# Values of two attention steps computed in one go in every second step, with four transposed-weight buffers and five MLP-input buffers

## The chip, the cores and the metric

The kernel runs on one core of a Trainium2 chip. The core has TensorE (PE, matrix products; PEld in the profile is its weight load), VectorE (DVE), ScalarE (ACT), GpSimd (POOL) and SyncE (SP), which here issues every DMA. The metric is the device time of one execution in microseconds (us), lower is better. The time before is the median of three runs.

## The reference

Two blocks follow each other. The first is attention with eight heads over a batch of eight, in which each query keeps only its 32 largest scores; the second is an MLP with a smooth ReLU.

```python
def _attn_ref(q, k, v):                   # (8, 8, 576, 64) each
    top_k = 32
    scores = scale * np.matmul(q, k.transpose(0, 1, 3, 2))
    kth = np.partition(scores, -top_k, axis=-1)[..., -top_k:-top_k + 1]
    scores = np.where(scores >= kth, scores, -1000000000.0)
    scores = scores - np.max(scores, axis=-1, keepdims=True)
    attn = np.exp(scores)
    attn = attn / (np.sum(attn, axis=-1, keepdims=True) + 1e-09)
    return np.matmul(attn, v).astype(np.float32)

def _moe_ref(x, w_in, w_out):             # (4608, 512), (512, 2048), (2048, 512)
    h = x @ w_in
    beta = 1.0
    neg = h <= -beta
    pos = h >= beta
    g = np.where(pos, h, np.where(neg, 0.0, (h + beta) ** 2 / (4.0 * beta)))
    return (g @ w_out).astype(np.float32)
```

Between them the attention's output is laid out as one row of 512 numbers (8 heads of 64) for each of the 8 x 576 tokens. Everything is float32.

## The kernel before

**Steps.** The attention is cut into 144 steps. One step takes a tile of 128 queries and two heads: 128 x 2 x 576 scores. A tile of queries needs four steps for its eight heads. The 576 queries of a batch element make four full tiles and a tail of 64; the tails of two batch elements share one tile of the MLP, and each tail takes two steps of four heads. The batch elements go in pairs: four tiles of the first, its tail, the tail of the second, four tiles of the second; so 36 steps a pair. A tile that has all its heads is a *chunk* for the MLP; there are 36 chunks.

**What one step does, engine by engine.** `scores` (L333) multiplies queries and keys on TensorE into PSUM (`sp`), and ScalarE evicts them to `s` (L352). VectorE finds the 32nd largest (`more`, `less`, MAX8 and MATCH_REPLACE8, L354 to L446) and multiplies the exponentials `e`, which ScalarE made (L388), with the mask (L451). GpSimd divides by the sum (L404). The weights must then be transposed, since the values are multiplied with the weights' columns on the partitions. In the early steps TensorE does it (`transpose_w`, L460); later `move_w` (L477) does it with DMAs: ScalarE splits the words into 16-bit halves (L481), SP writes them to DRAM (`rows`, L483) and reads them back transposed into a `wT` buffer (L484). There are three `wT` buffers. `values` (L490) multiplies values and `wT` on TensorE, 20 matmuls in the source (16 of `v_in`, 4 of the tail, as the profile counts them) into a PSUM tile `po`, and ScalarE copies `po` into `xT` (L511), the input of the MLP. When a chunk has its last values, `mlp` (L522) puts its pieces on a list.

**The MLP's pieces.** A chunk has eight pieces `hidden` (`ph`, L531: 16 matmuls in the profile for two blocks of hidden units; ScalarE makes `r` and `g` from `ph`, L535 and L542, GpSimd finishes `g`, L547 to L549) and sixteen `final` (`py`, L554), each four pieces behind its `hidden`. `ph` and `po` have one tag, so that both rotate through the same three PSUM buffers. `advance` (L625) puts pieces between the attention's instructions, as many as a planned share and a planned time of TensorE allow.

**Order.** The instructions on TensorE, VectorE, ScalarE and GpSimd stand exactly in the order in which this program issues them; each engine takes them in that order and waits where an operand is not ready or a buffer is not free. Only SP's order is the framework's. The main loop (L727) goes through steps `m` in seven slots. While the weights of the MLP are still being converted to the form in which the kernel keeps them (`early`, steps 0 to 8), other rules hold. Afterwards step `m` issues: in slot 1 the turning of queries for step `m + 3` (and in every second step a part of the next keys), in slot 2 the values of step `m - 3` and then the scores of step `m + 2`, in slot 3 the moving of the weights of step `m - 1`:

```python
                if slot == 2 and not early:
                    values_until(m - 2)
                if slot == (4 if early else 2):
                    begin_at(m + 2)
```

`values_until(x)` (L715) issues the values of all steps below `x` that are not issued yet. So before the change there is one set of values and one set of scores in each step, one behind the other on TensorE. The values of a chunk's last head pair always belong to an odd step.

**Buffers.** The pool `xtp` (L177) has six `xT`. A query tile is loaded into one of two `q_in`, and a tail into one `q_tl` of its own (L204 to L211). From the second batch pair on, queries are turned through DRAM as well: ScalarE makes `parts`, SP writes `lines` and reads them back transposed as `qT` or, for a tail, `qTt` (L272 to L279).

Of the kernel before, what the change touches and what calls it, by code (L numbers as in the profile page):

```python
# [11 lines left out]
F32 = mybir.dt.float32  # L12
# [14 lines left out]
def kernel(  # L27
# [11 lines left out]
    B, H, S, D = q.shape  # L39
    NTOK, DM = out.shape  # L40
    DFF = moe_w_in.shape[1]
    P = 128
# [6 lines left out]
    TL = S - SM  # L49
    assert 2 * TL == P  # L50
    SH = S // 2
    BLOCKS = 2 * NT + 1
# [121 lines left out]

    def run(ctx, paired):
        unit = 2.0 if paired else 1.0
        xtp = ctx.enter_context(tc.tile_pool(name="xtp", bufs=6))  # L177
        stage = ctx.enter_context(tc.tile_pool(name="stage", bufs=2))
        att = ctx.enter_context(tc.tile_pool(name="att", bufs=2))
        dram = ctx.enter_context(tc.tile_pool(name="dram", bufs=3, space=bass.MemoryType.DRAM))  # L180
# [3 lines left out]
        def whole(x, b):  # L184

            return x[b, :, 0:SM, :].rearrange("h (p c) d -> p h c d", c=NT)
# [17 lines left out]
        def load_queries(b, t):  # L204
            if t < NT:
                q_in = stage.tile([P, H, D], F32, name="q_in", bufs=2)
                nc.sync.dma_start(out=q_in, in_=whole(q, b)[:, :, t, :])
            else:
                q_in = stage.tile([TL, H, D], F32, name="q_tl", bufs=1)
                nc.sync.dma_start(out=q_in, in_=q[b, :, SM:S, :].rearrange("h p d -> p h d"))  # L210
            return q_in  # L211


        def main(i):
            return slice(0, SM) if i == 0 else slice(TL, S)

        def tail(i):
            return slice(SM, S) if i == 0 else slice(0, TL)
# [240 lines left out]

        def transpose_w(st):  # L460
            w = st["e"]
            st["wT"] = wT = (late or words).tile([P, BLOCKS, P], F32, name="wT", bufs=3 if late else 1)
            pt = ps.tile([P, 2, NT, P], F32, name="pw", tag="a", bufs=2)
            for i in range(2):
                for c in range(NT):
                    nc.tensor.matmul(pt[:, i, c, :], w[:, i, main(i)][:, c * P:(c + 1) * P], st["rz"][:, i, :],  # L466
                                     start=True, stop=True)
            for i in range(2):
                nc.scalar.copy(wT[:, i * (NT + 1):i * (NT + 1) + NT], pt[:, i])  # L469
            pt = ps.tile([P, P], F32, name="pwt", tag="a", bufs=2)  # L470
            for i in range(2):
                nc.tensor.matmul(pt[i * TL:(i + 1) * TL, :], w[:, i, tail(i)], st["rz"][:, i, :], start=True, stop=True)
            nc.scalar.copy(wT[:, NT], pt)
# [1 line left out]


        def move_w(st):  # L477
            st["wT"] = wT = late.tile([P, BLOCKS, P], F32, name="wT", bufs=3)
            halves = late.tile([P, 2, 2 * S], U16, name="halves")
            for i in range(2):  # L480
                nc.scalar.copy(halves[:, :, i * S:(i + 1) * S], st["e"][:, i, :].bitcast(U16).rearrange("p (k t) -> p t k", t=2))  # L481
            rows = dram.tile([P, 2, 2 * S], U16, name="rows")
            nc.sync.dma_start(out=rows, in_=halves)  # L483
            nc.sync.dma_start_transpose(wT.bitcast(U16), rows.rearrange("p t k -> (p t) k"))  # L484
# [31 lines left out]
        def rows_of(b, t):  # L516
            r0 = b * S
            if t < NT:
                return [(0, P, out[r0:r0 + SM, :].rearrange("(p c) n -> p c n", c=NT)[:, t, :])]
            return [(i * TL, (i + 1) * TL, out[r0 + i * S + SM:r0 + (i + 1) * S, :]) for i in range(2)]  # L520
# [74 lines left out]
        words, late = conversion.enter_context(tc.tile_pool(name="words", bufs=1)), None  # L595
# [19 lines left out]
        def inspect():  # L615
            nonlocal inspected
            if paired and inspected < n_pieces:
                inspect_piece(late, inspected)
                inspected += 1
# [67 lines left out]
        def begin_at(m):  # L687
            nonlocal pe_time
            if m < n:
                queries(m)  # L690
                begin(m)
                pe_time += 1.15
                scored[m] = pe_time + 2.0
# [21 lines left out]
        def values_until(m):  # L715
            nonlocal valued, pe_time
            while valued < min(m, n):
                pe_time = max(pe_time, ready_at[valued]) + 1.25
                values(state[valued])
                state[valued] = None  # L720
                if valued in ready:
                    ch = ready[valued]
                    mlp(xTs[ch], rows_of(*chunks[ch]), mlp_pool, ch == len(chunks) - 1)
                valued += 1

        first_late = None
        for m in range(n + 2):  # L727
            early = converted < n_pieces
            if not early and first_late is None:
                first_late = m  # L730
            elif not early and late is None:
                conversion.close()
                room.clear()
                late = ctx.enter_context(tc.tile_pool(name="late", bufs=1))

            share, left = (total - spent) / (n + 2 - m), sum(x[0] for x in pending)
            for r in sorted(ready):
                if r + 4 > m and r >= valued:
                    share = min(share, left / (r + 4 - m))
                    left += NK * NF + NF * DM // P  # L740
            top_k, parts = None, [0] * SLOTS
            if m < n:
                top_k = weights(state[m], state[m - 1] if m > 0 else None, state[m + 1] if m + 1 < n else None)
                parts = [1] * SLOTS if early else [1, 1, 0, 1, 1, 1, 1]
                start = max(dve_time, scored[m])
                now_converting = range(SLOTS)
                dve_time = start + K_TIME + PIECE_TIME * min(len(now_converting), n_pieces - converted)
                done[m] = dve_time
                state[m]["by_tensor"] = early or m >= n - 2
            for slot in range(SLOTS):  # L750
                now = start + (dve_time - start) * (slot + 1) / SLOTS
                for _ in range(parts[slot]):
                    next(top_k, None)
                if m < n and converted < n_pieces:
                    if slot in now_converting:
                        convert(now)
                elif slot == 3 and late is not None:
                    if m % 2:
                        inspect()
                    elif paired:  # L760
                        load(late, inspected, 1)
                if slot == 1 and 1 <= m <= n and state[m - 1]["by_tensor"]:
                    pe_time = max(pe_time, done[m - 1] + 2.0) + 1.0
                    transpose_w(state[m - 1])
                    ready_at[m - 1] = pe_time + 1.8
                if slot == 3 and 1 <= m <= n and state[m - 1] is not None and not state[m - 1]["by_tensor"]:
                    move_w(state[m - 1])
                    ready_at[m - 1] = done[m - 1] + 15.0
                if slot == 2 and m == n and paired:
                    judge(ps, att)  # L770
                if slot == 2 and (early or m == first_late or m >= n - 1):
                    values_until(m)
                if m == 0 and slot in (1, 2):
                    next(first)
                if slot == 2 and not early:
                    values_until(m - 2)
                if slot == (4 if early else 2):
                    begin_at(m + 2)
                if slot == (6 if early else 1):
                    queries(m + 3)  # L780
                    if (m < n and prep is None and next_keys < B and steps[m][0] == next_keys - 1 and steps[m][1] >= 1
                            and (next_keys > 1 or converted == n_pieces)):
                        prep = (turned_keys_of if next_keys > 1 else keys_of)(next_keys)
                    if prep is not None and (m % 2 == 0 or next_keys == 1):
                        got = next(prep, None)
                        pe_time += 0.5 if next_keys < 2 else 0.0
                        if got is None:
                            prep, next_keys = None, next_keys + 1
                        else:
                            keys[next_keys] = got  # L790
                advance((EARLY_SHARE if early else share) / SLOTS if m < n else 32.0, now)
            for _ in (top_k if top_k is not None else ()):
                pass
# [50 lines left out]
```

## Time and profile before

| | us |
|---|---|
| median of the runs | 1522.77 |
| all three runs | 1517.87, 1522.77, 1523.53 |
| the execution that was profiled | 1522.56 |
| its span, first to last instruction | 1520.5 |

The mean granted TensorE clock in the profiled execution is 0.981 of full speed. The stages are: up to about 130 us the MLP's weights are loaded and converted beside the first steps; from there to about 1440 us attention and MLP run side by side; the rest is MLP alone.

The costliest groups on each engine, from the same page (busy time, mean of one):

| engine, line, what | count | busy us | mean ns |
|---|---|---|---|
| PE L531 `ph` (hidden) | 4608 | 557.4 | 276 |
| PE L554 `py` (final) | 1152 | 550.7 | 603 |
| PE L351 `sp` (scores, 64x288) | 1024 | 163.6 | 436 |
| PE L498 `po` (values, `v_in`) | 2048 | 143.5 | 280 |
| DVE L372 MATCH_REPLACE8 | 864 | 375.0 | 437 |
| DVE L451 mask times `e` | 288 | 266.6 | 959 |
| POOL L404 division | 266 | 248.7 | 945 |
| POOL L549 end of `g` | 280 | 242.1 | 865 |
| ACT L481 `halves` | 266 | 293.6 | 1144 |

How to read it: a line of the timeline gives start and length of a run of equal instructions and, in brackets, the idle time of the engine before it with what ended that. Lengths of matmuls overlap, since matmuls are pipelined; the starts tell how long a group holds TensorE. A wait line gives total, count and longest. A line of windows gives the busy time of each engine in a stretch, with the number of instructions or groups in brackets, then the granted clock, the share of time in which the DMA engines moved data, and GB/s.

### The profile page before, as it was taken

Reading aid. Unit: us, or ns where it says so; the run is one execution under the profiler, and the core shown is the slowest. Engines: PE = TensorE matmul, PEld = TensorE weight load, DVE = VectorE, ACT = ScalarE, POOL = GpSimd, SP = SyncE. Lnnn points to the kernel's source line nnn. Section 1 sums busy time; section 2 is a strip of 40 time slices with the busy share of each in tenths; the row PEclk is TensorE's granted clock in tenths of the full one; section 3 lists DMA queues with packets and bytes.
Section 4 is the critical chain, followed back from the end, with each engine's and each line's share of the span. In section 5 each row is a group of like instructions: output and inputs, shape, how many; then the busy total and the mean of one; then the engine's idle time right before and its main releaser. Section 6 shows DMA issues by size and latency. Waiting matters only on the chain.

```text
span 1520.5 us, 32206 instructions
## 1 busy us (share of the span) xinstructions
PE 1450.9 (95%) x10625; PEld 1041.8 (69%) x10625; DVE 1422.2 (94%) x4424; ACT 1171.0 (77%) x2288; POOL 942.7 (62%) x1339
## 2 busy tenths in 40 slices
PE   5588999999999999999999999999999999999998
PEld 4466677677777767777777777666677677767675
DVE  6888999999999999999999999999999999999912
ACT  6896887787778888787778887787777887777732
POOL 4563656666666666666666665666666666666630
PEclk6798999999999999999999999999999999999999
DMA  9542567775577867886687868786576767655510
GB/s 250 167 135 70 135 164 182 198 193 157 159 196 200 205 171 185 226 209 168 173 198 186 200 168 197 206 216 173 161 192 187 203 164 190 158 156 151 140 31 17
DMA packets 512448, 259.76 MB, mean 171 GB/s; under 512 B 459152, under 2 KB 467344, under 8 KB 512272
## 3 DMA queue, kind: packets, MB, share of 16 engines
q1 hardware_dynamic: 512272, 257.62, 65.0%
q8 instruction: 86, 1.41, 0.4%
q14 instruction: 90, 0.74, 0.1%
HBM read 62.91 MB, written 102.04 MB: 108 GB/s over the span
## 4 chain that ended last, share of the span: by engine, by line
PE 83%; ACT 8%; DMA 5%; issue 2%; DVE 1%; POOL 0%; SPq 0%; ACTq 0%; POOLq 0%; DVEq 0%
PE py L554 31%; PE ph L531 29%; PE sp L351 10%; PE po L498 10%; DMA wT<-rows 2%; DMA rows<-halves 2%; PE pw L466 2%; ACT halves L481 2%; ACT e L388 1%; ACT units L145 1%; PE po L506 1%; ACT s L352 1%; ACT wT L469 1%; ACT raw L171 1%; DMA qTt<-lines 0%
## 5 line engine op out<-in xcount | busy, mean ns | idle before, releaser
L531 PEld LDWEIGHTS ph<-xT,w_in 128*128 128x128 f32 x4608 | 547.1, 192 | 101.7 <-issue 83.8
L531 PE MATMUL ph<-xT,w_in 128*128 128x128 f32 x4608 | 557.4, 276 | 3.2 <-POOL w_in L156 3.1
L554 PE MATMUL py<-w_out,g 128*128 128x512 f32 x1152 | 550.7, 603 | 0.0
L547 POOL TENSOR_SCALAR r<-r 128x256 f32<-128x256 f32 x276 | 159.9, 580 | 431.6 <-ACT r L535 431.5
L372 DVE MATCH_REPLACE8 more<-tops,more 128x288 f32<-128x288 f32 x864 | 375.0, 437 | 0.0
L554 PEld LDWEIGHTS py<-w_out,g 128*128 128x128 f32 x1152 | 198.1, 191 | 181.5 <-issue 160.4
L481 ACT COPY halves<-e 128x1152 uint16<-128x1152 uint16 x266 | 293.6, 1144 | 14.9 <-POOL e L404 8.9
L451 DVE SCALAR_TENSOR_TENSOR e<-s,kth,e 128x577 f32<-128x577 f32 x288 | 266.6, 959 | 2.0 <-ACT e L388 1.5
L549 POOL TENSOR_TENSOR g<-r,g 128x256 f32<-128x256 f32 x280 | 242.1, 865 | 22.0
L404 POOL TENSOR_SCALAR e<-e,rz 128x576 f32<-128x576 f32 x266 | 248.7, 945 | 0.0
L535 ACT ACTIVATE r<-ph,half 128x256 f32<-128x256 f32 (+1 forms) x296 | 136.4, 461 | 117.7 <-PE ph L531 84.5
L388 ACT ACTIVATE e<-s,nmax 128x576 f32<-128x576 f32 x288 | 222.5, 773 | 4.7
L352 ACT ACTIVATE s<-sp 128x576 f32<-128x576 f32 x288 | 172.5, 652 | 47.0 <-PE sp L351 44.7
L548 POOL TENSOR_TENSOR r<-r 128x256 f32<-128x256 f32 x276 | 190.0, 688 | 23.0
L351 PE MATMUL sp<-kT,qT 64*128 64x288 f32 x1024 | 163.6, 436 | 10.4 <-ACT kT L254 9.5
L498 PEld LDWEIGHTS po<-wT,v_in 128*64 128x64 f32 x2048 | 111.6, 137 | 75.0 <-ACT g L542 34.5
L498 PE MATMUL po<-wT,v_in 128*64 128x128 f32 x2048 | 143.5, 280 | 12.3 <-DMA wT<-rows 5.3
L542 ACT ACTIVATE g<-ph,minus 128x256 f32<-128x256 f32 x280 | 130.5, 466 | 0.0
L413 DVE MAX8 tops<-more 128x8 f32<-128x288 f32 x288 | 125.4, 443 | 0.0
L365 DVE TENSOR_TENSOR less<-s 128x576 f32<-128x576 f32 x144 | 123.9, 860 | 0.0
L351 PEld LDWEIGHTS sp<-kT,qT 64*128 64x128 f32 x1024 | 90.0, 189 | 46.6 <-issue 15.6
L365 DVE TENSOR_TENSOR more<-s 128x576 f32<-128x576 f32 x144 | 111.7, 775 | 10.5 <-ACT s L352 10.5
(88 smaller groups left out, 1379.3 us busy)
## 6 DMA issues: line engine op xcount, KB each, us to landing
rows<-halves SPq DMA_DIRECT2D x133, 576.0 KB, 3.1
lines<-parts SPq DMA_DIRECT2D x48, 256.0 KB, 2.7
q_in<-in_q_dram SPq DMA_DIRECT2D x32, 256.0 KB, 4.1
kT<-in_moe_w_in_dram SPq DMA_DIRECT2D x32, 256.0 KB, 3.1
v_in<-in_moe_w_out_dram SPq DMA_DIRECT2D x32, 256.0 KB, 3.0
v_in<-in_v_dram SPq DMA_DIRECT2D x32, 256.0 KB, 4.0
raw<-in_moe_w_in_dram SPq DMA_DIRECT2D x32, 256.0 KB, 3.1
out_dram<-y SPq DMA_DIRECT2D x32, 256.0 KB, 3.1
```

What stands on the lines that cost most here:

```text
L351: nc.tensor.matmul(*x, start=True, stop=True)
L365: nc.vector.tensor_tensor(out=x, in0=s[:, :, 0:SH], in1=s[:, :, SH:S], op=op)
L372: nc.vector.match_replace(out=st["rest"][:, i, :], in_to_replace=eight(st["tops"], i, r - 8), in_values=src[:, i, :], imm_value=LOWEST)
L388: nc.scalar.activation(e[:, i, :], s[:, i, :], AF.Exp, bias=nmax[:, i:i + 1])
L404: nc.gpsimd.tensor_scalar(st["e"][:, i, :], st["e"][:, i, :], rz[:, i:i + 1], 1.0, ALU.mult, ALU.mult)
L451: nc.vector.scalar_tensor_tensor(out=st["all"][1][:, i, :], in0=st["all"][0][:, i, :], scalar=last[i], in1=st["all"][1][:, i, :], op0=ALU. ...
L481: nc.scalar.copy(halves[:, :, i * S:(i + 1) * S], st["e"][:, i, :].bitcast(U16).rearrange("p (k t) -> p t k", t=2))
L498: nc.tensor.matmul(po[j * D:(j + 1) * D], v_in[:, h, c, :] if c < NT else v_tl[0][:, h, :], wT[:, block(j, c)], start=(c == 0), stop=(c == ...
L531: nc.tensor.matmul(ph[:, i], w_in[:, kk, f * P:(f + 1) * P], xT[:, kk], start=(kk == 0), stop=(kk == NK - 1))
L548: nc.gpsimd.tensor_tensor(out=r, in0=r, in1=r, op=ALU.mult)
L549: nc.gpsimd.tensor_tensor(out=g, in0=r, in1=g, op=ALU.add)
L554: nc.tensor.matmul(py[0], gs[f // group][:, f % group], w_out[:, f, :], start=(f == 0), stop=(f == NF - 1))
```

## The change

In the steps after the conversion, `values_until` gets `(m - 2) // 2 * 2` instead of `m - 2`. In an odd step nothing is issued by it; in an even step the values of step `m - 4` and of step `m - 3` are issued one behind the other. So the values of even steps come one step later than before, those of odd steps stand where they were. Since more weights are alive at a time, `wT` has four buffers (4.5 KB each per partition). To make room, `xT` has five buffers (2 KB each) and the tails' queries share the two buffers of `q_in` in place of one of their own (2 KB).

```diff
 def run(ctx, paired):
-        xtp = ctx.enter_context(tc.tile_pool(name="xtp", bufs=6))
+        xtp = ctx.enter_context(tc.tile_pool(name="xtp", bufs=5))
...
             else:
-                q_in = stage.tile([TL, H, D], F32, name="q_tl", bufs=1)
+                q_in = stage.tile([TL, H, D], F32, name="q_tl", tag="q_in", bufs=2)
                 nc.sync.dma_start(out=q_in, in_=q[b, :, SM:S, :].rearrange("h p d -> p h d"))
...
         def transpose_w(st):
             w = st["e"]
-            st["wT"] = wT = (late or words).tile([P, BLOCKS, P], F32, name="wT", bufs=3 if late else 1)
+            st["wT"] = wT = (late or words).tile([P, BLOCKS, P], F32, name="wT", bufs=4 if late else 1)
...
         def move_w(st):
-            st["wT"] = wT = late.tile([P, BLOCKS, P], F32, name="wT", bufs=3)
+            st["wT"] = wT = late.tile([P, BLOCKS, P], F32, name="wT", bufs=4)
...
                 if slot == 2 and not early:
-                    values_until(m - 2)
+                    values_until((m - 2) // 2 * 2)
```

## The prediction

> **What bounds the kernel now.** I read the totals and slices first, then the waits of TensorE and VectorE, then stretches of four steps, and last the timeline of single steps.
>
> ```profile
> PE 1450.9 (95%) x10625; PEld 1041.8 (69%) x10625; DVE 1422.2 (94%) x4424; ACT 1171.0 (77%) x2288; POOL 942.7 (62%) x1339
> ...
> PE   5588999999999999999999999999999999999998
> ...
> DVE  6888999999999999999999999999999999999912
> ```
>
> Two engines are full from the fourth slice (about 150 us) to the last two; there VectorE is done and TensorE works off the MLP alone. Which of the two sets the pace is seen in their waits.
>
> ```profile
> PE po L498 <- DMA wT<-rows: 5.3, 6, 1.3
> PE po L498 <- ACT g L542: 5.2, 6, 0.9
> ...
> PE sp L351 <- DMA qTt<-lines: 3.6, 2, 2.0
> ...
> DVE more L365 <- ACT s L352: 10.5, 10, 2.5
> ```
>
> These are totals, counts and the longest, in us. From 180 us to the last transposes TensorE waits some 15 us in all. VectorE's waits for scores (`more` from `s`) are scores that TensorE or the evicting ScalarE delivers late. In time order, those after 160 us come to 6.0 us, with two for `e` (0.2 and 1.35). So TensorE sets the pace, and VectorE has almost no reserve. Four steps at a time (columns: us, then the busy time of PE, PEld, DVE, ACT, POOL):
>
> ```profile
> 549.28:587.09 37.81, 36.22 (x292) 26.21 (x291) 37.81 (x121) 30.12 (x58) 24.07 (x34) 1.00 0.72 186
> 740.93:779.43 38.50, 38.50 (x273) 27.42 (x273) 38.50 (x121) 30.18 (x59) 26.26 (x36) 1.00 0.68 163
> 1033.87:1073.31 39.44, 38.55 (x273) 27.40 (x272) 38.67 (x121) 30.24 (x59) 26.02 (x37) 1.00 0.67 177
> ```
>
> VectorE's same 121 groups take 37.81, 38.50 or 38.67 us. It is elastic: least where TensorE stalls and POOL has less to do. In the third stretch one wait for a PSUM buffer costs TensorE 0.9 us per four steps. Now one step in the middle, TensorE alone (start, length, groups; starts are exact, lengths overlap):
>
> ```profile
> 819.41 1.95 PE L531 MATMUL ph<-xT,w_in 128*128 128x128 f32 x16
> 821.19 1.02 PE L554 MATMUL py<-w_out,g 128*128 128x512 f32 x2
> 822.15 1.09 PE L498 MATMUL po<-wT,v_in 128*64 128x128 f32 x16
> 823.07 0.39 PE L498 MATMUL po<-wT,v_tail 128*64 128x128 f32 x4
> 823.39 1.24 PE L351 MATMUL sp<-kT,qT 64*128 64x288 f32 x8
> 824.56 1.98 PE L554 MATMUL py<-w_out,g 128*128 128x512 f32 x4
> 826.38 5.52 PE L531 MATMUL ph<-xT,w_in 128*128 128x128 f32 x48
> ```
>
> The reader is to subtract starts. Two `py` matmuls take 0.86 us inside MLP work (0.43 each), but 0.96 here, before values: entering values costs 0.10. Values to scores is 1.24. Four `py` after scores take 1.82 instead of 1.72: leaving scores costs 0.10 too. There is no wait in these lines; it is the change of array shape (128\*128, 128\*64, 64\*128 in the lines).
>
> [...] the same `less` (L365) takes 0.74 us at 809.95 and 1.17 us at 799.90, beside POOL's `r` and `g`. [...]
>
> **The change part by part.** The orders of instructions of the two builds, set side by side, are the same on VectorE and POOL, and on TensorE and ScalarE too once the value matmuls and their `xT` copies are taken out. The MLP pieces keep their places. What moves is 65 values (those of even steps, from the odd step 15 of the order to step 143): each stands one step later, just ahead of the values of the odd step, with its copy beside the other copy.
>
> 1. *The pairing itself.* A lone value costs 0.10 (entry) + 1.24 = 1.34 us. Where it is taken away, MLP meets scores directly, which is a change of shape too: at 155.08 a `ph` group ahead of scores takes 1.88 instead of 1.78, so 0.10. Freed: 1.34 - 0.10 = 1.24. As the second of a pair it starts in the right shape. The end of the kernel shows that case:
>
> ```profile
> 1451.14 1.04 PE L498 MATMUL po<-wT,v_in 128*64 128x128 f32 x16
> 1452.02 0.39 PE L498 MATMUL po<-wT,v_tail 128*64 128x128 f32 x4
> 1452.24 1.04 PE L498 MATMUL po<-wT,v_in 128*64 128x128 f32 x16
> ```
>
> From 1451.14 to 1452.24 a value with values on both sides takes 1.10. Saved per pair: 1.24 - 1.10 = 0.14, times 65 = 9.1 us of TensorE.
>
> 2. *Waits for `wT`.* Four values at odd places of the order waited for their transpose: 0.67 (183.1), 0.76 (277), 1.02 (628) and 1.42 us (977), together 3.9. They get a step (9.6 us) more, so their own waits go. Next late is the partner's `wT`: at 283 and 634 it was late by 0.9 and 0.2 already, and now TensorE arrives earlier by what was saved. Bounds: 0 and 3.9; I take 1.0, since two of the four have such a neighbour. Four `wT` buffers instead of three: even `wT` reuse a buffer released one step earlier, odd ones as before. With three, the DMA queue would have waited for the delayed values; with four nothing gets later.
>
> 3. *The ring of `ph` and `po`.* The second `po` of a pair needs the `g` of the second of three `ph` ahead of it; in the row at 826.38 that `g` ends at 832.17, and as ScalarE now reaches it 1.2 us earlier, at about 830.9, ahead of the second value's start at about 831.8. Cost 0. The first `po` waits for the same `g` as before: the 0.9 us waits around 1000 to 1150 stay. If the cover fails, the price is at most that 0.9 for each of 32 such pairs, 29 us.
>
> 4. *ScalarE.* Copies wait for values on a queue that everything follows: in even steps the second copy stands ahead of the two evictions of `s`, but these scores come no later than before, since two steps together hold the same work. In odd steps the copy (and its wait, 1.27 us at 823.51) is gone from the queue. Cost 0, gain to VectorE: scores of odd steps come 1.2 us earlier.
>
> 5. *`q_tl` in the ring of `q_in`, five `xT`.* The load of the tile after the tails now waits for ScalarE's or TensorE's reading of the tails. Behind it on SP stand `rows` and `wT`. The late loads stand behind `lines<-parts`, which waits for the same reading; early, two loads wait for TensorE's transposes, with weight loads queued behind, several pieces ahead of need. Bounds -2 to +3, I take 0. `xT`: a tile is read within about six steps of its writing, the fifth comes 20 steps later; 0.
>
> 6. *VectorE's reserve.* The sum asks VectorE to shorten as well, since the last transposes (`pw`, 1441 to 1457) wait for its last weights. Its removable waits are 6.0 us; the rest must come from shorter blocking by POOL. The stretch at 549 shows 0.7 us less for four steps than the usual 38.50; the change asks for 2 x 0.14 = 0.28. Taken: it follows.
>
> Sum: -9.1 - 1.0 = -10.1; I keep 0.6 back for the final wait for VectorE's weights, so -9.5. The profiled execution took 1522.56 (span 1520.5 and 2.1 around it), 0.2 below the median of 1522.77. So 1513.
>
> **The rivals.**
>
> A. *VectorE does not follow.* Then only its waits are removed, 6.0 us less the lot that remains, and TensorE idles longer at the last transposes: 1516.5 to 1518. For: it is 100% busy in every middle stretch. Against: 37.81 above.
>
> B. *Most of it is absorbed.* TensorE's lead is spent at the tails (the scores at 562 and 912 wait 1.7 and 2.0 us for `qTt`) and at late `wT`, since those transfers, not TensorE, set the time there. Two such places in each of three batch pairs, at 1.5 us each (between the waits seen there), swallow 9: 1522.6 - 9.1 + 9 is near 1522, no change.
>
> C. *Slower: POOL's bursts meet VectorE's multiplication.* With values gone from odd steps, `r` and `g` start 1.2 us earlier in part of each pair. The weights' multiplication (L451) [...] takes 0.81 us free and 1.29 us blocked in the lines at 804 and 814. If in each of 65 pairs one more of four is blocked, VectorE gets 65 x 0.48 = 31 us longer, less 6.0 of waits and what TensorE saves in vain: about 1545; with half of them 1531. It decides from the point where four steps of VectorE exceed 38.5 us. Against: the blocked ones are as long for POOL, and over long stretches both engines kept one pace.
>
> The change not doing what it says is excluded by the orders.
>
> **How the numbers follow.** Main 0.47 (1509 to 1517), A 0.31 (1515 to 1519), B 0.10, C 0.12. From 0.5% on (7.6 us, about what a measurement of this kernel can tell from no change) it counts as faster: below 1515.2. Main gives that in nine of ten, A in a fifth: 0.48. Slower is C almost alone: 0.11. The rest, 0.41, is no change. For 8 in 10, the lower end takes part 2's bound and VectorE gaining more (1507), the upper end A and B whole (1523).
>
> **What would show it.** Right: value pairs with the second at 1.10 us after the first; TensorE's waits for `wT` near 2 us; VectorE's waits for `s` gone in the middle; four steps at about 38.2 us for both engines. Wrong: L451's mean above 0.96 us, or a wait of `po` for `g` longer than 5 us in all (part 3), or longer waits for `diag` at 1441 (A), or for `qTt` (B).

## The result and the profile after

The changed kernel took 1512.37 us (median of six, 1510.34 to 1516.81) against 1521.13 of the kernel before on the same chip: a ratio of 0.9937, 95% interval 0.9920 to 0.9955. A second set of six on another occasion gave 0.9928 (0.9909 to 0.9947). So the kernel became 0.6 to 0.7% faster, and 1513 was right to 0.1%. The profiled execution of the changed kernel, 1516.81 us with a span of 1514.6, is the slowest of its six, and so is that of the second set (1517.09). How large the waits below are in the quicker executions no trace shows.

The same parts of the page as before, totals and slices:

```profile
PE 1441.9 (95%) x10625; PEld 1042.8 (69%) x10625; DVE 1412.7 (93%) x4424; ACT 1167.1 (77%) x2288; POOL 921.8 (61%) x1339
...
PE   5588999999999999999999999899999999999998
...
DVE  7888999999999999999999999999999999999912
```

TensorE's busy time fell by 9.0 us and VectorE's by 9.5, with the same instructions. Four steps in the middle, from the view of stretches (us, then busy time of PE, PEld, DVE, ACT, POOL):

```profile
749.00:787.20 38.20, 38.20 (x275) 27.47 (x274) 38.20 (x121) 30.03 (x59) 24.84 (x36) 1.00 0.75 186
```

VectorE's 121 groups now take 38.20 where they took 38.50: it follows. By the starts of the scores, the period of four steps is 38.16 us instead of 38.46. TensorE's timeline shows where that comes from:

```profile
826.04 1.09 PE L498 MATMUL po<-wT,v_in 128*64 128x128 f32 x16
826.97 0.39 PE L498 MATMUL po<-wT,v_tail 128*64 128x128 f32 x4
827.19 1.04 PE L498 MATMUL po<-wT,v_in 128*64 128x128 f32 x16
828.06 0.39 PE L498 MATMUL po<-wT,v_tail 128*64 128x128 f32 x4
828.38 1.24 PE L351 MATMUL sp<-kT,qT 64*128 64x288 f32 x8
```

Subtract starts: from the first value to the scores the pair holds TensorE for 2.34 us, where two lone values took 2 x 1.24 = 2.48. The first gives way to the second after 1.15; there the array keeps its shape. The waits (total, count, longest) show what was given back:

```profile
PE pw L466 <- ACT diag L401: 24.5, 6, 5.3
...
PE po L498 <- ACT g L542: 15.3, 8, 5.9
...
ACT halves L481 <- DMA rows<-halves: 14.5, 8, 4.9
...
DVE more L365 <- ACT s L352: 11.9, 9, 2.6
...
PE po L506 <- DMA wT<-rows: 0.6, 1, 0.6
PE po L498 <- DMA wT<-rows: 0.6, 1, 0.6
```

TensorE's waits for `wT` fell from 5.3 us to 1.2, and those for `qTt` from 3.6 to 0.5, but its waits for `g` rose from 5.2 to 15.3. Five of the eight are of the old size, below 1 us; the three new ones (2.52, 2.56 and 5.87 us) stand behind the `ph` groups at about 278, 625 and 974 us, where SP loads keys and values for the batches to come. The longest, from three views of the changed kernel: SP, ScalarE, TensorE.

```profile
974.36 3.34 SPq L200 DMA_DIRECT2D v_tail<-in_v_dram  x5
977.80 0.55 SPq L483 DMA_DIRECT2D rows<-halves  x1
```

```profile
969.17 2.21 ACT L481 COPY halves<-e 128x1152 uint16<-128x1152 uint16 x2 [1.23 <-DMA rows<-halves]
...
976.93 0.19 ACT L171 ACTIVATION_READ_ACCUMULATOR raw<-raw,tiny 128x1 f32 x1
981.98 2.20 ACT L481 COPY halves<-e 128x1152 uint16<-128x1152 uint16 x2 [4.86 <-DMA rows<-halves]
```

```profile
974.25 5.52 PE L531 MATMUL ph<-xT,w_in 128*128 128x128 f32 x48
985.63 1.98 PE L498 MATMUL po<-wT,v_in 128*64 128x128 f32 x16 [5.87 <-ACT g L542]
```

There is one `halves` buffer. Its last contents were complete at 971.38 (969.17 + 2.21), but SP stores them only at 977.80, behind five loads of values' tails. ScalarE reaches the next copy at 977.12 (976.93 + 0.19) and stands still for 4.86 us, and the `r` and `g` behind that copy on its queue are what the first `po` of the pair waits for. Before the change, at the same place, SP and ScalarE:

```profile
980.18 1.96 SPq L200 DMA_DIRECT2D v_tail<-in_v_dram  x3
982.23 0.54 SPq L483 DMA_DIRECT2D rows<-halves  x1
```

```profile
974.92 2.19 ACT L481 COPY halves<-e 128x1152 uint16<-128x1152 uint16 x2
...
981.10 0.27 ACT L511 COPY xT<-po 128x128 f32<-128x128 f32 x1 [2.58 <-PE po L498]
...
986.75 2.19 ACT L481 COPY halves<-e 128x1152 uint16<-128x1152 uint16 x2
```

Two things differ. The first, and the larger at this place, is that ScalarE was later. Its copies came 11.8 us apart (starts at 974.92 and 986.75), and between them it had stood 2.58 us at 981.10 for the values of the odd step, which waited for `wT` (and 1.2 us for a `py`). After the change it is ready for the next copy 8.0 us after the start of the last (969.17 to 977.12): the wait for the values is gone from its queue, and it runs into the buffer instead.

The other is SP's own order, the only one that the program doesn't fix. Directly ahead of this store SP now issues five loads of tails where it issued three, and at 278 and 625 us four where it issued two. The traces of e1, e4 and e5 below, which have the pairing, show the new numbers; that of e2, which hasn't, shows the old ones. The two more loads hold SP for 1.4 to 1.8 us, and ScalarE's waits at the three places are 2.8, 2.9 and 4.9 us. At 625 us they are the larger part: ScalarE is ready for its next copy after 9.2 us there, where 10.2 lay between copies before. Why the order comes out so isn't known.

A second price can hang on a long wait. In stretches after that one, the column behind the busy times is the granted clock of TensorE:

```profile
985.60:987.80 2.20, 2.17 (x20) 2.17 (x22) 2.20 (x11) 1.94 (x4) 2.04 (x4) 0.50 1.05 289
987.80:989.40 1.60, 1.60 (x24) 1.44 (x20) 1.14 (x5) 0.70 (x3) 1.44 (x4) 0.74 0.97 393
989.40:991.50 2.10, 2.10 (x12) 1.18 (x11) 0.06 (x1) 1.55 (x4) 2.02 (x5) 1.00 0.23 89
```

TensorE comes back at half clock, and this pair of values takes 3.78 us instead of 2.34.

The kernel before pays this price too, at the last transposes. Both kernels wait there for 2.12 us. Before (first line), the restart was slow, with a granted clock of 0.50 from 1448.0 to 1449.5 us; after (second line), it isn't:

```profile
1446.20 3.04 PE L466 MATMUL pw<-diag,e 128*128 128x128 f32 x16 [2.12 <-ACT diag L401]
```

```profile
1440.48 2.05 PE L466 MATMUL pw<-diag,e 128*128 128x128 f32 x16 [2.12 <-ACT diag L401]
```

From here to the second value behind it, the kernel before needs 4.94 us (1446.20 to 1451.14). Where nothing is slow or late, this takes 3.35: 2.25 up to the first value, as in the change (1440.48 to 1442.73), and 1.10 for that value, as in the prediction. So the slow restart cost 1.6 us.

The account of the profiled executions: 65 pairs at 0.15 are -9.8; `wT` -4.1; `qTt` -3.1; `g` +10.1; the slow restarts at 634 and 986 +3.1; the one at 1446 that is gone -1.6. Together -5.4, where the spans differ by -5.9. The last term can't be credited to the change: of the runs below, e10 restarts slowly there though it has the pairing, and e9 doesn't though it lacks it.

The rival of POOL's bursts is answered by VectorE's multiplication, on the page (count, then busy us and mean ns, then the idle time ahead of it):

```profile
L451 DVE SCALAR_TENSOR_TENSOR e<-s,kth,e 128x577 f32<-128x577 f32 x288 | 251.8, 909 | 3.6 <-ACT e L388 3.5
```

Its mean fell from 959 to 909 ns. Of the 288, 60 took over 1.0 us, where 90 did before, and each of these ran beside an instruction of POOL; those that ran while POOL stood idle took at most 0.82 us, in both traces. So it was not held up beside POOL more often.

### The profile page after: what moved, and what is told of

Same layout as the page of the kernel before. It is cut to its first block, busy times and chain, and to the rows that moved or that the text cites. A ratio compares the mean times of both kernels' runs of the same rounds, so it can differ in the third digit from the quotient of the medians.

```text
span 1514.6 us, 32180 instructions
## 1 busy us (share of the span) xinstructions
PE 1441.9 (95%) x10625; PEld 1042.8 (69%) x10625; DVE 1412.7 (93%) x4424; ACT 1167.1 (77%) x2288; POOL 921.8 (61%) x1339
## 4 chain that ended last, share of the span: by engine, by line
PE 85%; ACT 8%; DMA 2%; issue 2%; POOL 1%; DVE 0%; SPq 0%; ACTq 0%; POOLq 0%; DVEq 0%
PE py L554 32%; PE ph L531 30%; PE sp L351 10%; PE po L498 10%; PE pw L466 2%; ACT halves L481 1%; ACT e L388 1%; ACT units L145 1%; PE po L506 1%; DMA rows<-halves 1%; ACT s L352 1%; DMA wT<-rows 1%; ACT wT L469 1%; ACT raw L171 0%; ACT g L542 0%
## 5 line engine op out<-in xcount | busy, mean ns | idle before, releaser
L451 DVE SCALAR_TENSOR_TENSOR e<-s,kth,e 128x577 f32<-128x577 f32 x288 | 251.8, 909 | 3.6 <-ACT e L388 3.5
L549 POOL TENSOR_TENSOR g<-r,g 128x256 f32<-128x256 f32 x280 | 227.8, 814 | 22.0
L404 POOL TENSOR_SCALAR e<-e,rz 128x576 f32<-128x576 f32 x266 | 223.4, 850 | 0.0
L498 PE MATMUL po<-wT,v_in 128*64 128x128 f32 x2048 | 143.4, 281 | 17.3 <-ACT g L542 15.3
L498 PEld LDWEIGHTS po<-wT,v_in 128*64 128x64 f32 x2048 | 117.0, 140 | 52.4 <-ACT g L542 40.1
```

Of the source, the lines that this page charges most:

```text
L404: nc.gpsimd.tensor_scalar(st["e"][:, i, :], st["e"][:, i, :], rz[:, i:i + 1], 1.0, ALU.mult, ALU.mult)
L451: nc.vector.scalar_tensor_tensor(out=st["all"][1][:, i, :], in0=st["all"][0][:, i, :], scalar=last[i], in1=st["all"][1][:, i, :], op0=ALU. ...
L498: nc.tensor.matmul(po[j * D:(j + 1) * D], v_in[:, h, c, :] if c < NT else v_tl[0][:, h, :], wT[:, block(j, c)], start=(c == 0), stop=(c == ...
L549: nc.gpsimd.tensor_tensor(out=g, in0=r, in1=g, op=ALU.add)
```

## The experiments

Theory 1: what pays is that two values stand side by side, with fewer changes of array shape. Theory 2: what pays is the buffers and the later places that they allow. Each time below is compared with the kernel before, run on the same chip; intervals are 95%.

**e1_pair_only** takes the new call of `values_until` alone.

```diff
-                    values_until(m - 2)
+                    values_until((m - 2) // 2 * 2)
```

> Only the pairing of the values; three buffers of transposed weights, six of the MLP's inputs and the last query tile's own buffer stay as before. Theory 1 (each pair of values back to back saves about 0.15 us of changes of array shape, 65 pairs, 9.8 us): 0.993 to 0.995 of before, second values of a pair near 1.10 us, L451 near 910 ns. Theory 2 (the gain came with the buffers and the later queue positions): 0.998 to 1.002. If the fourth buffer of transposed weights is needed by the pairing, the halves wait on the ACT or the wT waits of TensorE grow by some 1 to 2 us in each of many places, and the time is 1.00 or above.

Measured: 0.9952 (0.9934 to 0.9969). The period of four steps in the middle is 38.16 us, as with the whole change, and L451's mean 916 ns. The waits for `g` came to 16.1 us, those of ScalarE for `halves` to 16.7, those for `wT` to 2.4. Those for `qTt` fell to 0.8. So the pairing alone brings the effect, less at most a fraction of a per cent, and the fourth `wT` buffer isn't what makes it work.

**e2_bufs_only** keeps the buffers of the change and the old call.

```diff
-                    values_until((m - 2) // 2 * 2)
+                    values_until(m - 2)
```

> Only the buffers of the change; values one step at a time as before. Theory 1: 0.998 to 1.002, and a four-row period of 38.46 us as before. Theory 2: 0.993 to 0.996.

Measured: 0.9992 (0.9980 to 1.0003), and a period of 38.46 us. Theory 2 falls as far as the buffers go; the later places of the values are e3's part. The waits for `qTt` are gone here too. So the buffers remove them, probably by `q_tl` in the ring of `q_in`; but e1, without this ring, has only 0.8 us of them, so the pairing removes most of them by itself. The waits for `wT` are 6.1 us here, and no gain is left.

**e3_apart** delays the same values as the change, with the same buffers, but puts a piece of the MLP between the two.

```diff
-                if slot == 2 and not early:
-                    values_until((m - 2) // 2 * 2)
+                if slot in (1, 2) and not early and m % 2 == 0:
+                    values_until(m - 4 + slot)
```

> The buffers of the change and the same delay of every second value, but the two values of an even step are kept apart by a unit of the MLP, so that the array changes shape as often as before. Theory 1: the gain is gone, 0.999 to 1.005. Theory 2 (what pays is the delay and the slack it gives): 0.993 to 0.996, as the whole change.

Measured: 1.0154 (1.0130 to 1.0177). The direction is Theory 1's, the size isn't: 24 us slower than before, not at most 8. TensorE's timeline shows both parts of it:

```profile
444.28 2.05 PE L531 MATMUL ph<-xT,w_in 128*128 128x128 f32 x16
446.27 1.09 PE L498 MATMUL po<-wT,v_in 128*64 128x128 f32 x16
...
463.33 1.09 PE L498 MATMUL po<-wT,v_in 128*64 128x128 f32 x16
464.25 0.39 PE L498 MATMUL po<-wT,v_tail 128*64 128x128 f32 x4
464.57 1.13 PE L554 MATMUL py<-w_out,g 128*128 128x512 f32 x2
465.63 1.09 PE L498 MATMUL po<-wT,v_in 128*64 128x128 f32 x16
```

A value between MLP work takes 1.24 (463.33 to 464.57), and the piece between two values is dearer by 0.2: sixteen `ph` take 1.99 instead of 1.78, two `py` 1.06 instead of 0.86, one 0.10 each for leaving and for entering the values' shape. So I had miscounted: against the kernel before, each pair has one exit and one entry more, about 0.2 us, or 65 x 0.2 = 13 us in all. To this comes a wait that only this order has: a `ph` behind the early value finds its PSUM buffer still being read for `g`.

```profile
1199.97 0.39 PE L498 MATMUL po<-wT,v_tail 128*64 128x128 f32 x4
1201.80 1.38 PE L531 MATMUL ph<-xT,w_in 128*128 128x128 f32 x10 [1.44 <-ACT g L542]
```

These waits come to 25.3 us in 17. Against that, the waits of `po` for `g` (5.2 us), for `wT` (5.3) and for `qTt` (3.1 of 3.6) are gone. That makes +24.7, and the spans differ by 27.0. The run shows that the delay doesn't pay in this order. What delay alone would be worth it can't tell, and it measures the shapes only through its starts.

**e4_halves2** is the whole change with two `halves` buffers, and three of `wT` to make room.

```diff
-            st["wT"] = wT = late.tile([P, BLOCKS, P], F32, name="wT", bufs=4)
-            halves = late.tile([P, 2, 2 * S], U16, name="halves")
+            st["wT"] = wT = late.tile([P, BLOCKS, P], F32, name="wT", bufs=3)
+            halves = late.tile([P, 2, 2 * S], U16, name="halves", bufs=2)
...
```

> The whole change with two buffers for the weights' halves and three of transposed weights instead of one and four. If the ACT's wait for the single halves buffer (14.5 us in 8 waits) is what makes TensorE wait for g (15.3 us in 8), both fall to under 4 us and the time is 0.988 to 0.991 of before. If those waits only stand in for the late transfer of the next wT, TensorE waits for wT<-rows as long as it did for g, and the time is 0.993 to 0.995, as the change. If the fourth wT is needed, over 0.995.

Measured: 0.9953 (0.9938 to 0.9967). ScalarE's waits for `halves` are gone and TensorE's for `g` back at 5.2 us, but at the same places it now waits for the next transfer. TensorE's timeline:

```profile
980.40 1.09 PE L498 MATMUL po<-wT,v_in 128*64 128x128 f32 x16 [0.89 <-ACT g L542]
981.33 0.39 PE L498 MATMUL po<-wT,v_tail 128*64 128x128 f32 x4
985.15 1.97 PE L498 MATMUL po<-wT,v_in 128*64 128x128 f32 x16 [3.44 <-DMA wT<-rows]
```

The first value runs, and the second finds its `wT` missing, with the half clock behind it again (1.97 for 1.09). By the expectation, a ratio over 0.995 would also fit that the fourth `wT` is needed. The trace speaks against it here: the copy into `halves` was complete at 969.8, the store stands on SP at 976.90, and the transposing read behind it waits 3.0 us for that store. So the buffer is where the lateness shows, not where it comes from. That leaves SP, which stores `rows` behind its loads.

**e5_change_again** is the change itself, in one set with the next three.

> The whole change once more, beside the next three on the same chip. Theory 1: 0.992 to 0.9955, PE waits for g of 9 to 16 us, longest 3 to 6 us, at the steps where the values' small tails are loaded (about 278, 625 and 974 us).

Measured: 0.9928 (0.9909 to 0.9947), 1513.67 us; waits for `g` 15.1 us in 8, longest 6.3, just over the range expected.

**e6_tails_act** issues the loads of the values' tails (two of L196, four of L200 for each batch from the third on) on ScalarE's queue. ScalarE's order is fixed, and so is their place now; their transfers run at other times too (the first four of L200 at 324 us; SP had issued its own between 246 and 279). **e11_tails_act_again** repeats it.

```diff
...
-                nc.sync.dma_start(out=v_tl[1][g * TL:(g + 1) * TL, 2 * hp:2 * hp + 2, :],
+                (nc.sync if b < 2 else nc.scalar).dma_start(out=v_tl[1][g * TL:(g + 1) * TL, 2 * hp:2 * hp + 2, :],
```

> The whole change, with the small loads of the values' tails (6 for each batch from the third on) issued on the ACT's queue instead of SP's; the computation is the same. If these loads, issued on SP ahead of rows<-halves, are what makes the weights late at about 278, 625 and 974 us, the waits for g at L498 fall from about 15 us to 5 (those of 0.9 us stay) and the time is 0.988 to 0.990, some 6 to 8 us below the change; the ACT's six issues for each batch cost TensorE nothing. If the lateness is that of the transfers themselves (the loads' bytes, the wait of wT for its rows, the key block's loads), it stays within 0.001 of the change.

> The change with the tails' loads on the ACT's queue once more, beside the two others on one chip: 0.986 to 0.989, waits for g at L498 of 5 us in 6.

Measured: 0.9876 (0.9858 to 0.9894), 1504.59 us, 9.1 below the change in the same set; the repeat 0.9887 (0.9868 to 0.9906). The waits of e6:

```profile
DVE more L365 <- ACT s L352: 5.6, 3, 2.5
...
PE po L498 <- ACT g L542: 5.2, 6, 0.9
...
PE po L498 <- DMA wT<-rows: 1.5, 2, 0.9
```

ScalarE's waits for `halves` are down to 0.6 us. Taking those six loads a batch out of SP's queue thus gives back all that the pairing had lost: spans of 1504.5 and 1520.5 differ by 16.0, and the account (pairs -9.8, `wT` -3.8, `qTt` -3.1, +1.4 of a new wait, -1.6 for the restart at the end) makes -16.9. Whether it is their place ahead of the stores or their traffic beside them, this run can't tell; e12 is about that. It isn't free on ScalarE, though the expectation said so: in two batches its queue stands at these loads, for 8.6 us, and TensorE waits 1.4 us (2.3 in the repeat) for the `xT` behind.

**e7_tails_act_h2** adds e4's two `halves` and three `wT` to e6.

> As e6_tails_act, with two buffers of halves and three of transposed weights. With the tails off SP's queue neither halves nor wT should wait: waits of the ACT for rows<-halves under 3 us, of TensorE for wT under 2 us, time within 0.001 of e6_tails_act. If the single halves buffer costs something by itself, it is 0.001 to 0.003 lower than e6.

Measured: 0.9877 (0.9858 to 0.9896), as e6. With the loads off SP, the single `halves` buffer costs nothing. Three `wT` cost nothing in time either, though TensorE's waits for `wT` are 2.6 us, over the 2 us expected.

**e8_triple** puts three values back to back in every third step.

```diff
-                    values_until((m - 2) // 2 * 2)
+                    values_until((m - 2) // 3 * 3)
```

> As the change, but three values back to back in every third step instead of two in every second. Theory 1: a second and a third value of a group cost 1.09 us each after a first of 1.24, so per step 0.10 us is saved instead of 0.075: 130 steps, 3.3 us less than the change, 0.991 to 0.992, if nothing is later. Rival: three values in a row need three free po buffers and three wT that have landed, so TensorE waits for g or wT in every third step, 0.5 us or more each, 43 groups, 20 us or more: 1.005 or above.

Measured: 1.0069 (1.0047 to 1.0091). From the starts in its trace a group of three takes 3.43 us where nothing is late, where Theory 1 asks for 1.24 + 2 x 1.09 = 3.42. But the kernel is 20 us slower than the change. The rival's number came true, but not its reason: TensorE waits only 5.0 us for `g` and 3.0 for `wT`. A wait that neither named is for turned queries: scores wait 9.5 us for `qT<-lines` and 5.1 for ScalarE's copies into `qT`. The chain of waits has another look (the chain of the changed kernel is 85% PE):

```profile
PE 42%; DVE 42%; ACT 8%; issue 4%; DMA 2%; POOL 1%; SPq 0%; POOLq 0%; ACTq 0%; DVEq 0%
```

Between 700 and 870 us scores follow each other after 6.6 to 12.7 us instead of 8.4 to 10.8, and VectorE carries 42% of the chain. The last scores start at 1422.8 us, as in the change (1423.1), but TensorE has had gaps by then and has 108 us of MLP left instead of 91. Why the pieces fall so unevenly I didn't test.

**e9_before_tails_act** is the kernel before with e6's edit alone.

> The kernel before with the tails' loads on the ACT's queue, nothing else. If the tails' place on SP cost the kernel before only its waits for wT at those places (3.9 us in four, of which 0.9 us each may stay as waits for g), 0.9975 to 0.9995; the pairing then is worth 0.989 to 0.991 with the loads out of the way (e6 against this one), its full 9.8 us and more. If the move pays by something else (ACT's queue as such, less on SP everywhere), the kernel before gains as much as the change did, 6 us or more: under 0.996.

Measured: 1.0065 (1.0040 to 1.0090), slower, which neither expectation foresaw. On ScalarE:

```profile
894.67 6.47 ACTq L200 DMA_DIRECT2D v_tail<-in_v_dram  x4
901.19 0.27 ACT L511 COPY xT<-po 128x128 f32<-128x128 f32 x1 [6.48 <-DMA v_tail<-in_v_dram]
```

The four issues take 0.6 us each, as on SP, but with gaps of up to 2.8 us between them, and a copy of `xT` that TensorE is about to need stands behind. What ScalarE waits for between them the trace doesn't name. That happens in three batches (17.8 us on ScalarE, 7.3 on TensorE), and the waits for `wT` rose to 8.9 us. Why `wT` is later here with less on SP, while it is earlier in e6, I can't say. So e6's edit isn't a gain by itself; it pays in the paired rhythm.

**e10_pair_only_tails_act** is e1 with e6's edit.

> Only the pairing and the tails' loads on the ACT's queue: three buffers of transposed weights, six of the MLP's inputs, the last query tile in its own buffer, as before the change. If the change's buffers are worth nothing, 0.987 to 0.989, as e6_tails_act. If the fourth wT or the shared query buffers carry part of e6's gain, 0.990 or above, with TensorE waiting for qTt at about 560 and 910 us (1.7 and 2.0 us) or the ACT for rows<-halves.

Measured: 0.9919 (0.9900 to 0.9938), 1511.61 us, against 1508.22 of e11 in the same set. TensorE waits once for `qTt` (1.6 us) and 3.7 us for `xT`. So the buffers seem to carry some 0.2 to 0.4% once the loads are out of the way, but the intervals overlap slightly.

**e12_rows_act** leaves the loads on SP and issues `rows<-halves` on ScalarE's queue, directly behind the copies.

```diff
-            nc.sync.dma_start(out=rows, in_=halves)
+            nc.scalar.dma_start(out=rows, in_=halves)
```

> The whole change, with rows<-halves of every step issued on the ACT's queue right behind its two copies, where SP's loads cannot hold it up; the tails' loads and wT<-rows stay on SP. If the late issue of rows<-halves behind the loads is what holds the halves buffer (13.7 to 16.7 us in 7 to 9 waits of the ACT so far), those waits fall under 4 us, the waits for g at L498 to about 5 us, and the time to 0.987 to 0.990, unless 110 more issues of 0.35 us delay the ACT's s and e by more than they save. If the store itself is slow because other transfers share the engines, the halves waits stay above 8 us and the time within 0.002 of the change (0.993).

Measured: 1.0234 (1.0201 to 1.0267). ScalarE waits for `halves` not once, though SP still issues the tails' loads at these places (three at 1001.18, the store at 1004.78). The read behind that store waits for it and starts at 1007.59, so the buffer was free at most 5.0 us after the copy began (1002.57); in the change, ScalarE was ready for the next copy after 8.0. So what held the buffer was the late issue on SP, and not the traffic. The price is ScalarE's:

```profile
442.56 2.19 ACT L481 COPY halves<-e 128x1152 uint16<-128x1152 uint16 x2
444.77 0.34 ACTq L483 DMA_DIRECT2D rows<-halves  x1
445.16 0.60 ACT L557 ACTIVATE y<-py 128x512 f32<-128x512 f32 x1 [0.42 <-ACT halves L481]
```

Behind the copy ScalarE now has a gap of 0.42 us, and the issue itself, which isn't counted as busy, takes 0.34 of it. Without the issue, the next instruction starts 0.10 us before the end of the copy (in the change: 969.17 + 2.21 against 971.28). The 125 such gaps of the trace (ahead of `e`, `r` and `y`) come to 53.3 us. The scores' way through ScalarE and the turning of queries suffer, and the waits for `g` fall only to 12.7 us, not to 5:

```profile
DVE more L365 <- ACT s L352: 51.4, 46, 5.0
...
PE sp L351 <- DMA qT<-lines: 32.0, 16, 4.6
...
PE po L498 <- ACT g L542: 12.7, 18, 1.4
```

## Why the prediction was right, and where not

*The time.* 1513 forecast, 1512.4 measured: it was the main case, and its main term carried it. That it came so close is partly luck, since the smaller terms were wrong in opposite directions: in the profiled execution, `wT` and `qTt` gave 6.2 us more than was taken, and the waits for `g`, with the half clock behind them, cost 13.2 that were taken at 0. Against that execution alone the change is -5.75 us for the -9.5 forecast.

*The first reading.* A slice is 38 us, so both engines are full from the fifth slice (152 us) on, not from the fourth. And of the two waits for `qTt` that rival B counts with, the first is 1.6 us, not 1.7. Neither bears on the sum.

*Part 1, the pairing.* 0.14 us a pair was forecast, from a place at the end of the kernel where two values stood side by side, and 0.15 was measured. The second value starts after 1.15 us, not 1.10, and itself takes 1.19 instead of 1.24, which is the same sum. e1 and e2 put the gain on the pairing; e3 and e8 show the same price of a change of shape from other orders: 0.10 us for each change in e3, and 3.43 us for three values in e8.

*Part 2, `wT`.* A saving of 1.0 us was taken, and 4.1 was measured (5.3 to 1.2); the list of signs, with waits near 2 us, was nearer than the sum. The reason given for the fourth buffer isn't borne out: with three (e1) the waits for `wT` are 2.4 us, and the ratio can't be told from the change's.

*Part 3, the ring of `ph` and `po`: this is the step that failed.* "The first `po` waits for the same `g` as before: the 0.9 us waits around 1000 to 1150 stay." They stayed, but the sum for `g` went from 5.2 to 15.3 us (the sign of being wrong was set at 5, which the kernel before passed already), and three waits were 2.5 to 5.9 us long where 0.9 was the most allowed for one. The step asked when ScalarE reaches `g` in an ordinary row and took from it that it is never later. It left out what stands ahead of `g` on ScalarE in the rows where SP loads values: the copy into `halves`, waiting for a store that SP has not issued. The orders were set side by side for four engines, and SP's, which the pairing changes, was not among them. e12 shows that the issue is what's late, e4 that another buffer only hands the wait on to `wT`, e6 that without the loads on SP both are gone and 9 us come back.

*Parts 4 and 5.* Scores of odd steps came earlier, but VectorE's waits for `s` in the middle did not vanish: 2.5 us at about 640 and 991 are new, behind the same stoppage, and so is most of one of 3.3 for `e` at 985. `q_tl` in the ring was costed at 0 between -2 and +3. The waits for `qTt` went from 3.6 to 0.5 us; e2 lost them by the buffers, e1 all but 0.8 by the pairing, so the gain can't be booked to the ring alone.

*Part 6 and rival A.* VectorE followed; the waits for `diag`, 24.7 us before, are 24.5, so rival A doesn't hold. *Rival C*'s figure, L451's mean, went down from 959 to 909 ns. *Rival B* had the right places, the steps with the next batch's transfers, and a sum of that size (9 us; here 10.1 of waits for `g` plus 3.1 of half clock), but in the change the wait shows at `g` and neither at `qTt` nor at `wT`; only e4 has it at `wT`. What it didn't see is that the removed waits there would pay for part of it.

The combination of the change with e6's edit, at 1504.59 us, beats both kernels.

## What to carry to other kernels

Where TensorE sets the pace, put matmuls of one array shape side by side: here each pair gave 0.15 us, and it counted although VectorE was equally full. That doesn't go on without end: three side by side made this kernel slower. When a step gets shorter, look on the in-order queue of each helping engine for the instruction that runs into a single buffer next, and from there to the queue that must free it; here another buffer only moved such a wait. Where a queue's order is the framework's, compare it before and after too: it can change with an edit elsewhere. Moving a load to another engine's queue has to be priced as work of that engine: the same edit gave 9 us in one rhythm and cost 8.5 in another.

## What the runs showed of the hardware that was not expected

- After some waits TensorE's matmuls came back at a granted clock of 0.50, at once or within about 1 us, for some 3 to 5 us in all, which cost another 1.4 to 2.5 us: after 2.12 us (at 1446 before the change), 2.56 (at 634 in the change), 3.44 (at 985 in e4) and 5.87 (at 986 in the change). After 2.52 us (at 286 in the change), 2.72 (at 288 in e5) and 2.00 (at 912 before it) the clock stayed at 1.00. The wait at the last transposes is the plainest case: it is 2.12 or 2.13 us in eleven of the traces, and the 16 matmuls behind it are slow (3.04 to 3.57 us) in four (before, e2, e3, e10) and take 2.05 us in seven (the change, e1, e5, e6, e9, e11, e12). So in these runs the length of a wait alone doesn't decide, and the traces don't say what does.
- The same six loads, issued on ScalarE's queue, stood there with gaps in some batches and without in others: the four of L200 took 2.9 us from first to last in one batch of e6 and 5.1 in another. The traces don't say what the gaps wait for.
